# HGRN recurrence and top-k capacity routing on one core: identity products, gate weights, candidate lists and zero writes rearranged

## The chip, the cores and the metric

The kernel runs on one core of one Trainium2 chip. The metric is the device time of one launch in microseconds (us); lower is better. A core has TensorE (PE, with its weight loads PEld), VectorE (DVE), ScalarE (ACT), GpSimd (POOL), and SyncE (SP), which here only issues DMAs; the transfers are done by 16 DMA engines.

## The reference

```python
sig = 1.0 / (1.0 + np.exp(-f_logit))                    # x, f_logit: (4, 5056, 256)
f = lower_bound + (1.0 - lower_bound) * sig
for t in range(S):                                      # per batch row and channel
    h = f[:, t] * h + (1.0 - f[:, t]) * x[:, t]
    y[:, t] = h
x = y.reshape(20224, 256)
logits = x @ w_gate                                     # 8 experts
expert_idx = argmax(logits);  gate_w = softmax(logits)[expert_idx]
out = zeros((20224, 256))
for e in range(8):
    tok_idx = the 80 tokens of expert e with the largest gate_w
    out[tok_idx] = gate_w[tok_idx] * (relu(x[tok_idx] @ w1[e]) @ w2[e])
```

w1 is (8, 256, 1024) and w2 is (8, 1024, 256), all in float32. At most 640 of 20224 rows of the output are not zero, so nearly all of the 20.7 MB that are written are zeros.

## The kernel before

**Scan stage.** A unit n (0 to 39) is 512 time steps of one batch row; a group g is the four batch rows of the same 512 steps, so there are ten groups, and unit n belongs to group n // 4. `OLD = 8` is the last group but one, `LAST = 39` the last unit. The loop at L410 is software-pipelined, and each engine works through its instructions in the order in which the loop emits them. For a unit: `load` (L246) issues two DMAs of 512 KB on SP, f_logit and x, into rings of four buffers; `gate` takes the sigmoid in place on ACT; `enter` multiplies x by it on POOL (unit 0 on DVE); `to_channels` turns both into channel-major PSUM tiles with TensorE transposes ("sp" for f, "up" for x); `decay` writes the decay factors to `h_all` on ACT; `scan` runs two recurrences on DVE, in place in `h_all`; `logits` multiplies by the gate weights `wg`, which `gates` (L242) has scaled once by 1 - lower_bound on DVE.

**Group steps.** Some units after a group is complete, `of_group` hands out its steps one unit at a time: `aside` copies the logits from PSUM on ACT, `by_token` transposes them on TensorE, `maxima` takes the maximum over experts and the difference from it on DVE (tile `cand`), `choice` finds the first best expert on DVE (tiles `eq`, `pick`) and marks it. The last two groups are handled by hand at L423 to L469: `exponentials` on ACT, `halved` (sums over experts by halving, POOL), `worth` (gm = mark minus sum, POOL or DVE), `candidates` (transpose on TensorE, copy on ACT), and `peaks`, which takes the best 8 of each list with MAX8 on DVE. There are `NP` = 8 lists of 128 columns per partition, one per pair of old groups and parity, and the 256 columns of the last two groups are kept whole, so that `fresh` has 64 + 256 = 320 columns.

**Selection.** From L537 DVE takes the best 16 of `fresh`, `spread` and the `rivals` products compare them across partitions, ACT (`signs`, 8 passes) and DVE (two index searches, then `beat`, 4 passes) count who is larger, and the products into `kept` put the 80 tokens of each expert in order. Then ACT, DVE and POOL gather the chosen columns of `h_all`.

**Experts.** `weights` (L492) loads w1 and w2 in halves of 512 KB, 32 of them, into a ring of six, which take the place of the load buffers in memory; the first six are issued at L505. `steps` does 70 steps: a step s below 64 does four matmuls of `hidden` (s = 8 e + c), and from step 6 on also the products of `result` for s - 6. Weight k (from 2 on) is first used at step 2k + 2. Each used-up weight calls `more(1)`, which issues the next weight on SP and then some zeros; the m-th call falls at step 2m + 3 (from the third on) and issues weight m + 5.

**Zeros.** `first_zeros` writes 8 rows per partition (1 MB) from a zeroed tile; it is issued at n = -1. All other zeros are copied inside the output in DRAM by `clear_some(m)`, in quarters of 32 partitions (256 KB); 76 quarters are listed. Before, 20 quarters go out beside the scans at n = 4 to 35, 6 at n = 36 (behind the last load), 30 between the first six weights, and 20 with `more`, the last of them with its 16th call. `scatters` holds back the writes of the experts' rows until all zeros are issued.

**Identity products.** `busy(pool, m, tag)` (L178) issues m products of the identity with itself, two matmul rows of the profile each, into a tile that nobody reads.

On every engine the order of the code is the order of the work: what waits on SP, say, stands in front of all DMAs that the code issues later.

Of the kernel before, what the change touches and what calls it, by code (L numbers as in the profile page):

```python
# [35 lines left out]
def kernel(  # L36
# [94 lines left out]
    parts = [(g, g * P + i) for g in range(0, OLD, 2) for i in range(2)]  # L131
# [26 lines left out]
    def first_zeros(zero):  # L158
        m = ZR * D // ZC
        nc.sync.dma_start(out=out_z[:, :ZR * D].rearrange("p (m z) -> p m z", m=m),  # L160
                          in_=zero.unsqueeze(1).broadcast_to([P, m, ZC]))
# [40 lines left out]
    with tc.tile_pool(name="ld", bufs=4) as ld, \  # L202
# [6 lines left out]
        def setup():  # L209
# [26 lines left out]
            busy(psu, 16, "up")  # L236
# [5 lines left out]
        def gates():  # L242
            for o in range(DC):
                nc.vector.tensor_scalar_mul(wg[:, o], wg[:, o], omlb[:, ds(o, 1)])
# [57 lines left out]
        def aside(g):  # L302
            k = run(g)
            ls = lss[g] = gsm.tile([P, B, P], F32, name="ls", tag="ls")
            if k < P:
                nc.gpsimd.memset(ls[:, :, k:], 0.0)
            nc.scalar.copy(ls[:, :, :k], lgs.pop(g)[:, :, :k])  # L307
# [25 lines left out]
        def choice(g, engine):  # L333
# [5 lines left out]
            nc.vector.tensor_reduce(pick, eq, AX.X, ALU.max)  # L339
            engine.tensor_tensor(marks[:, g], eq, pick.unsqueeze(2).broadcast_to(full),  # L340
                                 ALU.subtract)

# [45 lines left out]
        def peaks(g, tops):  # L388
            for i, (g0, lo) in enumerate(parts):
                if g0 == g:  # L390
                    nc.vector.max(out=tops[:, ds(i * TOP, TOP)], in_=cand[:, lo:(g + 2) * P:2])
# [16 lines left out]
        HALF = OLD // 2  # L408

        for n in range(-AHEAD, n_unit):  # L410
# [3 lines left out]
            elif n == -1:  # L414
                first_zeros(zero)
# [4 lines left out]
            unit(lambda m: to_channels(m, sts, sps, pss, "sp", False), n + 1)  # L420
            unit(lambda m: to_channels(m, uts, ups, psu, "up", True), n + 1)
            unit(decay, n + 1)
            if n == LAST - 2:  # L423
                aside(OLD)
                exponentials(0, OLD)
            elif n == LAST - 1:
                for k in range(0, OLD, HALF):
                    halved(k, HALF)
            unit(scan, n)
            if n == 0:  # L430
                gates()
            some_of(of_group, 1 if n != LAST - 1 else 0)
            unit(logits, n - 1)
            if n + AHEAD == LAST:
                clear_some(6)
            elif B <= n < LAST - AHEAD and (n % 2 or n >= n_unit - 3 * B):
                clear_some(1)
            if n > 0 and n % B == 0:
# [430 lines left out]
```

## Time and profile before

| | us |
|---|---|
| median of 3 runs | 227.79 (226.98 to 228.44) |
| the profiled execution, its own time | 226.11 |
| its span, first to last instruction | 224.2 |
| busy: PE / PEld / DVE / ACT / POOL | 194.8 / 165.1 / 157.7 / 131.6 / 139.8 |
| DMA moved | 80.55 MB, mean 359 GB/s |

The span is 1.9 us shorter than the execution's own time. Busy time is an average over stages with different limits, so the rows further down are taken stage by stage. The stages are: scans to about 129 us, selection to 156 us, experts to 217 us, and the last rows' way out to 224 us.

### The profile page before, as it was taken

The page shows a single profiled execution, that of the slowest core. Times are in us where ns is not written, and L with a number is a line of the kernel's source. Part 1 is how long each engine was busy: PE and PEld are TensorE (multiplying, and loading weights), DVE is VectorE, ACT ScalarE, POOL GpSimd, SP SyncE. Part 2 cuts the span into 40 slices and gives each one's busy share as a digit, 9 for nine tenths or more (in the row PEclk, how much of TensorE's full clock was granted, in tenths as well). Part 3 has the DMA queues.
Part 4 walks back from the last instruction along what each step waited for, and adds up shares of the span by engine and source line. Part 5 has one row for each costly group of instructions (what it writes and reads, how often), then busy time and mean ns, then how long its engine had stood idle before and what let it go on. Part 6 is the DMA issues. An engine that isn't in the chain of part 4 may idle for free.

```text
span 224.2 us, 5701 instructions
## 1 busy us (share of the span) xinstructions
PE 194.8 (87%) x1938; PEld 165.1 (74%) x1938; DVE 157.7 (70%) x487; ACT 131.6 (59%) x367; POOL 139.8 (62%) x279
## 2 busy tenths in 40 slices
PE   7977899998999999999697868989998978989970
PEld 7855678786878787878485648978986856778850
DVE  5398679999999999999978867935686744420010
ACT  4546988879898888877668540428655335330100
POOL 3456988989898989887677760107967710039220
PEclk9999999999999999999999999999999999999998
DMA  6999999999999999999999299999698999999800
GB/s 227 341 417 415 420 420 415 417 421 417 419 416 421 417 421 417 422 415 425 414 418 386 91 324 392 385 361 398 201 292 319 408 400 411 399 379 378 284 21 23
DMA packets 28794, 80.55 MB, mean 359 GB/s; under 512 B 3027, under 2 KB 11349, under 8 KB 26453
## 3 DMA queue, kind: packets, MB, share of 16 engines
q1 hardware_dynamic: 28368, 79.45, 91.3%
q0 software_dynamic: 384, 0.66, 0.8%
q8 instruction: 17, 0.28, 0.5%
q14 instruction: 21, 0.16, 0.2%
q10 hardware_dynamic: 4, 0.00, 0.0%
HBM read 78.39 MB, written 21.36 MB: 445 GB/s over the span
## 4 chain that ended last, share of the span: by engine, by line
DMA 44%; PE 31%; ACT 11%; DVE 4%; POOL 3%; issue 2%; SPq 1%; POOLq 1%; ACTq 0%; DVEq 0%
DMA f_t<-in_f_logit_dram 21%; DMA w_sb<-in_moe_w_dram 11%; DMA x_t<-in_x_dram 9%; PE warm L181 7%; PE h_ps L707 6%; PE y_ps L722 6%; PE sp L266 5%; ACT h_all L276 4%; DMA out_dram<-out_dram 3%; ACT f_t L255 3%; PE lg L299 3%; PE up L266 3%; ACT ls L307 2%; ACT signs L565 2%; POOL xe L675 1%
## 5 line engine op out<-in xcount | busy, mean ns | idle before, releaser
L259 POOL TENSOR_TENSOR x_t<-f_t,x_t 128x1024 f32<-128x1024 f32 x39 | 93.5, 2401 | 21.3 <-DMA x_t<-in_x_dram 14.7
L284 DVE TENSOR_TENSOR_SCAN h_all<-h_all,up 128x512 f32<-128x512 f32 (+1 forms) x80 | 94.6, 1240 | 3.8 <-ACT h_all L276 2.5
L276 ACT ACTIVATE h_all<-sp,nomlb 128x512 f32<-128x512 f32 (+1 forms) x80 | 50.0, 676 | 7.9 <-PE sp L266 7.7
L255 ACT ACTIVATE f_t<-f_t 128x1024 f32<-128x1024 f32 x40 | 42.5, 1062 | 19.9 <-DMA f_t<-in_f_logit_dram 19.5
L266 PE MATMUL up<-ident,x_t 128*128 128x128 f32 x320 | 42.4, 276 | 6.3 <-POOL x_t L259 5.6
L707 PEld LDWEIGHTS h_ps<-xt,w_sb 128*128 128x128 f32 x256 | 37.0, 191 | 12.4 <-issue 5.2
L266 PE MATMUL sp<-ident,f_t 128*128 128x128 f32 x320 | 43.8, 280 | 1.5 <-ACT h_all L276 1.5
L266 PEld LDWEIGHTS up<-ident,x_t 128*128 128x128 f32 x320 | 35.3, 140 | 10.1 <-POOL x_t L259 9.3
L266 PEld LDWEIGHTS sp<-ident,f_t 128*128 128x128 f32 x320 | 34.4, 141 | 9.5 <-issue 6.9
L707 PE MATMUL h_ps<-xt,w_sb 128*128 128x80 f32 x256 | 36.5, 268 | 4.9 <-DMA w_sb<-in_moe_w_dram 3.9
L722 PE MATMUL y_ps<-w_sb,hid 128*80 128x256 f32 x128 | 37.3, 381 | 0.0
L675 POOL COPY xe<-h_all 128x8 uint8 x192 | 26.2, 197 | 12.8 <-issue 8.2
L299 PE MATMUL lg<-h_all,wg 128*32 128x128 f32 (+1 forms) x640 | 26.5, 282 | 4.3 <-ACT ls L307 3.1
L675 DVE COPY xe<-h_all 128x8 uint8 x256 | 20.9, 162 | 11.4 <-issue 11.3
L181 PE MATMUL warm<-ident 128*128 128x128 f32 x188 | 24.9, 298 | 1.4 <-POOL ident masks.py:199 1.4
L181 PEld LDWEIGHTS warm<-ident 128*128 128x128 f32 x188 | 24.3, 213 | 1.7 <-POOL ident masks.py:199 1.4
L716 ACT ACTIVATE hid<-h_ps 128x320 f32<-128x320 f32 x16 | 7.0, 437 | 31.1 <-PE h_ps L707 28.4
L740 POOL DMA_INDIRECT out_dram<-y,goal x8 | 7.6, 951 | 28.0 <-DMA w_sb<-in_moe_w_dram 18.8
L299 PEld LDWEIGHTS lg<-h_all,wg 128*32 128x32 f32 x640 | 15.4, 108 | 11.3 <-ACT ls L307 5.1
L675 ACT COPY xe<-h_all 128x8 uint8 x192 | 20.2, 193 | 5.4 <-issue 3.4
L722 PEld LDWEIGHTS y_ps<-w_sb,hid 128*80 128x80 f32 x128 | 14.8, 152 | 0.8
L737 DVE TENSOR_SCALAR y<-y_ps,gsl 80x256 f32<-80x256 f32 x8 | 3.8, 476 | 16.2 <-PE y_ps L722 16.2
(125 smaller groups left out, 97.2 us busy)
## 6 DMA issues: line engine op xcount, KB each, us to landing
f_t<-in_f_logit_dram SPq DMA_DIRECT2D x40, 512.0 KB, 6.6
x_t<-in_x_dram SPq DMA_DIRECT2D x40, 512.0 KB, 6.8
w_sb<-in_moe_w_dram SPq DMA_DIRECT2D x32, 512.0 KB, 7.9
out_dram<-out_dram SPq DMA_DIRECT2D x35, 256.0 KB, 7.1
out_dram<-out_dram SPq DMA_DIRECT2D x4, 1024.0 KB
out_dram<-out_dram SPq DMA_DIRECT2D x6, 512.0 KB, 14.8
out_dram<-out_dram SPq DMA_DIRECT2D x3, 768.0 KB
out_dram<-zero SPq DMA_DIRECT2D x1, 1024.0 KB
```

Source lines behind the costliest of these rows:

```text
L181: nc.tensor.matmul(warm, ident, ident, start=True, stop=True)
L255: nc.scalar.activation(s_t, s_t, ACT.Sigmoid, scale=-1.0)
L259: (nc.gpsimd if n else nc.vector).tensor_tensor(u_t, sts[n], u_t, ALU.mult)
L266: nc.tensor.transpose(at, src[n][:, r, ds(o * P, P)], ident)
L276: nc.scalar.activation(columns(n, o).rearrange("c (p r) -> c p r", r=R), sps.pop((n, o)).rearrange("c (r p) -> c p r", r=R) [:, lead(n // ...
L284: nc.vector.tensor_tensor_scan(h, h, ups.pop((n, o))[:, lead(n // B):], columns(n - B, o)[:, size(n // B - 1) - 1:] if n >= B else 0.0, AL ...
L299: nc.tensor.matmul(lgs[g][ds(r * LC, LC), b, :k], wg[:, o], h[:, r], start=o == 0, stop=o == DC - 1, skip_group_check=True)
L675: copy(xe[:, :, ds(WORD * (k + j), WORD)], pair(v - HOME))
L707: nc.tensor.matmul(HP[e, i][:, c], w[1, e, i][:, o, ds(c * P, P)], XT[e][:, o], start=o == 0, stop=o == DC - 1, skip_group_check=True)
L716: nc.scalar.activation(HID[e][:, ds(i * CH, CH)], HP.pop((e, i)), ACT.Relu)
L722: nc.tensor.matmul(YP[e], HID[e][:, c], w[2, e, c // CH][:, c % CH], start=c == 0, stop=c == FC - 1)
L740: one = nc.gpsimd.indirect_dma_start(out=out, out_offset=bass.IndirectOffsetOnAxis(ap=goal[:, ds(e, 1)], axis=0), in_=Y.pop(e), in_offset= ...
```

## The change

Nine edits, by the diff:

- The identity products fall from 16 to 9 at the start (`setup`), from 4 to 3 ahead of the last group's transposes, and from 32 to 10 ahead of the selection; 20 and 22 stay where they were.
- `gates` runs on ACT in place of DVE, and is emitted at n = -1 in place of n = 0.
- `first_zeros` is cut into four quarters, emitted at n = 0 to 3, behind that turn's load.
- Beside the scans a quarter goes out at every third unit, n = 5, 8, ... 35: 11 in place of 20.
- Behind the last load (n = 36) 10 quarters in place of 6.
- Between the first six weights 5, 5, 6, 6, 6, 6 in place of 5 each: 34 in place of 30. With `more` one each, so 21 in place of 20 are left for it, the last with the 21st call.
- Group OLD: its `aside` moves from n = 37 to 36, its `by_token` between the transposes of n = 37, its `maxima` behind the scan of n = 37. Its mark goes to POOL, its sums to DVE (before: `halved` on POOL).
- The last group: `aside` in two parts, three units ahead of the last logits and one behind. All four `worth` of old groups on POOL, half of `halved` put off to there, and the order of `candidates`, `by_token` and `peaks` is new.
- Four lists of 256 columns (one per half of the old groups and parity) in place of eight of 128; `fresh` has 288 columns.

```diff
     assert OLD % 4 == 0 and size(OLD) == G and OLD == n_grp - 2
-    parts = [(g, g * P + i) for g in range(0, OLD, 2) for i in range(2)]
+    HALF = OLD // 2
+    parts = [(g, g * P + i) for g in range(0, OLD, HALF) for i in range(2)]
     NP = len(parts)
...
     zeros = [(k, q) for k in clears[1:] for q in range(ZQ)]
-    def first_zeros(zero):
+    def first_zeros(zero, q=0, n=ZQ):
         m = ZR * D // ZC
-        nc.sync.dma_start(out=out_z[:, :ZR * D].rearrange("p (m z) -> p m z", m=m),
-                          in_=zero.unsqueeze(1).broadcast_to([P, m, ZC]))
+        rows = ds(q * QP, n * QP)
+        nc.sync.dma_start(out=out_z[rows, :ZR * D].rearrange("p (m z) -> p m z", m=m),
+                          in_=zero[rows].unsqueeze(1).broadcast_to([n * QP, m, ZC]))
     def clear(k, q=0, m=ZQ):
...
             nc.vector.tensor_tensor(before, before, mates, ALU.mult)
-            busy(psu, 16, "up")
+            busy(psu, 9, "up")
             lb_t = plg.tile([P, DC], F32, name="lb_t", tag="lt")
...
             for o in range(DC):
-                nc.vector.tensor_scalar_mul(wg[:, o], wg[:, o], omlb[:, ds(o, 1)])
+                nc.scalar.activation(wg[:, o], wg[:, o], ACT.Identity, scale=omlb[:, ds(o, 1)])
         def load(n):
...
                                      start=o == 0, stop=o == DC - 1, skip_group_check=True)
-        def aside(g):
+        def aside(g, lo=0, hi=B):
             k = run(g)
-            ls = lss[g] = gsm.tile([P, B, P], F32, name="ls", tag="ls")
-            if k < P:
-                nc.gpsimd.memset(ls[:, :, k:], 0.0)
-            nc.scalar.copy(ls[:, :, :k], lgs.pop(g)[:, :, :k])
+            if lo == 0:
+                lss[g] = gsm.tile([P, B, P], F32, name="ls", tag="ls")
+                if k < P:
+                    nc.gpsimd.memset(lss[g][:, :, k:], 0.0)
+            nc.scalar.copy(lss[g][:, lo:hi, :k], lgs[g][:, lo:hi, :k])
         def by_token(g):
...
             maxima(g)
-        def choice(g, engine):
+        def chosen(g):
             eq = gsm.tile([P, C, E], F32, name="eq", tag="eq")
...
             nc.vector.tensor_reduce(pick, eq, AX.X, ALU.max)
+            return eq, pick
+
+        def mark(g, eq, pick, engine):
             engine.tensor_tensor(marks[:, g], eq, pick.unsqueeze(2).broadcast_to(full),
                                  ALU.subtract)
+
+        def choice(g, engine):
+            mark(g, *chosen(g), engine)
         def exponentials(g0, g1, aside=False):
...
                 if g0 == g:
-                    nc.vector.max(out=tops[:, ds(i * TOP, TOP)], in_=cand[:, lo:(g + 2) * P:2])
+                    nc.vector.max(out=tops[:, ds(i * TOP, TOP)], in_=cand[:, lo:(g + HALF) * P:2])
         def unit(f, m):
...
         LAST = n_unit - 1
-        HALF = OLD // 2
         for n in range(-AHEAD, n_unit):
...
                 nc.sync.dma_start(out=wg[:, :, :E], in_=w_gate.rearrange("(o p) e -> p o e", p=P))
-            elif n == -1:
-                first_zeros(zero)
+            elif 0 <= n < ZQ:
+                first_zeros(zero, n, 1)
             if n == -AHEAD:
...
             unit(lambda m: to_channels(m, sts, sps, pss, "sp", False), n + 1)
+            if n == LAST - 2:
+                by_token(OLD)
             unit(lambda m: to_channels(m, uts, ups, psu, "up", True), n + 1)
             unit(decay, n + 1)
-            if n == LAST - 2:
-                aside(OLD)
+            if n == -1:
+                gates()
+            elif n == LAST - 2:
                 exponentials(0, OLD)
             elif n == LAST - 1:
-                for k in range(0, OLD, HALF):
-                    halved(k, HALF)
+                halved(0, HALF)
             unit(scan, n)
-            if n == 0:
-                gates()
-            some_of(of_group, 1 if n != LAST - 1 else 0)
+            if n == LAST - 2:
+                maxima(OLD)
+            some_of(of_group, 1)
             unit(logits, n - 1)
+            if n == LAST - 3:
+                aside(OLD)
             if n + AHEAD == LAST:
-                clear_some(6)
-            elif B <= n < LAST - AHEAD and (n % 2 or n >= n_unit - 3 * B):
+                clear_some(10)
+            elif B < n < LAST - AHEAD and n % 3 == 2:
                 clear_some(1)
-            if n > 0 and n % B == 0:
+            if n > 0 and n % B == 0 and n // B <= OLD:
                 g = n // B - 1
-                of_group += ([[lambda g=g: aside(g)]] if g < OLD else [])
-                of_group += [[lambda g=g: shifted(g)], [lambda g=g: choice(g, nc.gpsimd if g < OLD else nc.vector)]]
+                of_group += [[lambda g=g: aside(g)], [lambda g=g: shifted(g)],
+                             [lambda g=g: choice(g, nc.gpsimd)]]
         assert not of_group
+        g = n_grp - 1
+        aside(g, 0, B - 1)
+        best = chosen(OLD)
         exponentials(OLD, OLD + 1)
         logits(LAST)
-        g = n_grp - 1
-        aside(g)
-        busy(psu, 4, "up")
+        aside(g, B - 1, B)
+        worth(0, 0, 2, nc.gpsimd)
+        worth(2, 0, 2, nc.gpsimd)
+        mark(OLD, *best, nc.gpsimd)
+        sums(OLD, OLD + 1)
+        candidates(0)
+        busy(psu, 3, "up")
+        candidates(2)
         by_token(g)
-        for k in (0, 2, HALF):
-            worth(k, k // HALF * HALF, 2, nc.gpsimd)
-        worth(OLD - 2, HALF, 2, nc.vector)
-        for k in (0, 2, OLD - 2, HALF):
-            candidates(k)
+        halved(HALF, HALF)
+        worth(HALF, HALF, 2, nc.gpsimd)
+        worth(HALF + 2, HALF, 2, nc.gpsimd)
+        worth(OLD, OLD, 1, nc.gpsimd)
         assert OLD == 8
...
         choice(g, nc.vector)
-        halved(OLD, 1)
-        worth(OLD, OLD, 1, nc.gpsimd)
-        turned(OLD, 1, fresh[:, ds(NP * TOP, P)])
+        candidates(HALF)
         sums(g, g + 1)
         worth(g, g, 1, nc.vector)
+        candidates(HALF + 2)
+        turned(OLD, 1, fresh[:, ds(NP * TOP, P)])
         turned(g, 1, fresh[:, ds(NP * TOP + P, P)])
-        busy(psu, 32, "up")
-        for k in (2, OLD - 2, HALF):
-            peaks(k, fresh)
+        busy(psu, 10, "up")
+        peaks(HALF, fresh)
         nc.scalar.copy(cand[:, OLD * P:], fresh[:, NP * TOP:])
...
         w_sb[key] = weights(*key)
-        clear_some(5)
+        clear_some(6 if len(w_sb) > 2 else 5)
     far = consts.tile([K, E], F32, name="far")
...
                     w[key] = weights(*key)
-                    clear_some(1 + (len(late) % 4 == 0))
+                    clear_some(1)
                 del late[:m]
...
```

## Rows read from the trace of the kernel before

**Rows 1.** Chain that ended last, shares of the span by engine.

```profile
DMA 44%; PE 31%; ACT 11%; DVE 4%; POOL 3%; issue 2%; SPq 1%; POOLq 1%; ACTq 0%; DVEq 0%
```

**Rows 2.** Windows: stretch, us, busy PE PEld DVE ACT POOL, clock, DMA share, GB/s.

```profile
20.00:94.00 74.00, 69.94 (x865) 58.49 (x866) 68.52 (x75) 61.91 (x85) 64.49 (x33) 1.00 1.02 418
94.00:122.00 28.00, 24.35 (x293) 19.55 (x291) 25.84 (x28) 19.81 (x28) 21.46 (x11) 1.00 1.03 420
...
124.00:128.00 4.00, 3.54 (x70) 2.94 (x72) 3.90 (x6) 2.64 (x4) 2.51 (x5) 1.00 0.10 29
128.00:157.00 29.00, 24.45 (x222) 22.62 (x219) 19.32 (x87) 11.79 (x73) 10.11 (x49) 1.00 1.01 371
157.00:160.00 3.00, 3.00 (x28) 2.96 (x28) 2.23 (x26) 2.94 (x28) 3.00 (x24) 1.00 0.35 97
160.00:172.00 12.00, 11.55 (x82) 9.70 (x80) 9.07 (x94) 6.20 (x46) 9.12 (x67) 1.00 0.89 294
172.00:198.00 26.00, 22.10 (x149) 17.96 (x150) 13.06 (x138) 10.88 (x86) 6.61 (x48) 1.00 1.05 404
```

**Rows 3.** Timeline of the start: start us, us, engine, line, operation, tiles, count.

```profile
1.41 6.66 PE L181 MATMUL warm<-ident 128*128 128x128 f32 x32 [1.41 <-POOL ident masks.py:199]
...
8.40 1.22 DVE L259 TENSOR_TENSOR x_t<-f_t,x_t 128x1024 f32<-128x1024 f32 x1
...
12.68 1.71 DVE L244 TENSOR_SCALAR wg<-wg,omlb 128x32 f32<-128x32 f32 x2
...
15.77 1.06 ACT L255 ACTIVATE f_t<-f_t 128x1024 f32<-128x1024 f32 x1 [3.26 <-DMA f_t<-in_f_logit_dram]
```

**Rows 4.** Timeline of one group's scans, and line L335 (min/median/max ns).

```profile
55.63 0.29 DVE L325 TENSOR_REDUCE mx<-lt 128x16 f32<-128x128 f32 x1 [0.51 <-PE lt L313]
...
59.15 5.96 DVE L284 TENSOR_TENSOR_SCAN h_all<-h_all,up 128x512 f32<-128x512 f32 x5
...
L335 DVE SCALAR_TENSOR_TENSOR eq<-cand,revexp x10: 264/666/1719, 36.0 to 133.3; 128x128 f32<-128x128 f32 x10
```

**Rows 5.** Timeline, end of the scans: last x product, group OLD's maxima, last scans.

```profile
122.04 2.36 POOL L259 TENSOR_TENSOR x_t<-f_t,x_t 128x1024 f32<-128x1024 f32 x1 [0.61 <-DMA x_t<-in_x_dram]
...
124.07 0.29 DVE L325 TENSOR_REDUCE mx<-lt 128x16 f32<-128x128 f32 x1 [1.28 <-PE lt L313]
...
124.60 4.25 DVE L284 TENSOR_TENSOR_SCAN h_all<-h_all,up 128x448 f32<-128x448 f32 x4
```

**Rows 6.** Timeline of SP: first weight, and the first weight behind a used-up one.

```profile
126.53 0.38 SPq L496 DMA_DIRECT2D w_sb<-in_moe_w_dram  x1
...
158.36 0.37 SPq L500 DMA_DIRECT2D w_sb<-in_moe_w_dram  x1
```

**Rows 7.** Timeline of the selection: identity products, MAX8 lists, rivals, ranks.

```profile
135.26 7.31 PE L181 MATMUL warm<-ident 128*128 128x128 f32 x64
135.46 1.99 DVE L391 MAX8 fresh<-cand 128x8 f32<-128x128 f32 x6 [0.42 <-PE fresh L380]
...
138.03 0.50 DVE L542 MAX8 vals<-fresh 128x8 f32<-128x320 f32 x1 [0.58 <-ACT last_of L472]
...
139.75 0.36 DVE L550 TENSOR_TENSOR spread<-vals,place 128x192 f32<-128x192 f32 x1
...
142.41 0.82 PE L555 MATMUL rivals<-spread,mates 128*128 128x192 f32 x4
...
147.29 0.17 DVE L586 COPY rank<-by_act 128x8 f32<-128x8 f32 x1 [1.65 <-ACT signs L565]
```

**Rows 8.** Chain that ended last, in order of time: start us, us, what.

```profile
156.32 2.90 PE h_ps L707 x24
...
197.67 0.64 PE h_ps L707 x4
...
214.24 3.04 PE y_ps L722 x14
```

**Rows 9.** Windows (columns as in the second group), TensorE idle at the end.

```profile
222.00:223.00 1.00, 0.00 (x0) 0.00 (x0) 0.00 (x0) 0.00 (x0) 0.00 (x0) 0.70 0.00 0
```

## The prediction

> **What bounds the kernel now.** I read the chain of waits first: DMA holds 44% of it, TensorE 31%, and DVE, the busiest engine beside TensorE in the scans, only 4% [rows 1]. Then the windows by stage [rows 2]. In the scans the DMA share is full and the rate is 418 to 420 GB/s, while DVE is busy 68.52 of 74 and 25.84 of 28 us: transfers set the pace, with DVE close behind. From 124 to 128 the DMA engines are nearly empty (29 GB/s): the last load and the six quarters behind it are through, and the first weight is not issued until 126.53 [rows 6], because it takes over load buffers that the transposes of unit 39 still read. From 128 to 157 they are full again at 371 GB/s with six weights and 30 quarters. From 157 to 160 they are nearly empty (97), to 172 half fed (294), then full (404) to 198. In that last stretch TensorE waits for weights; the last such wait ends at 197.67, and from there it runs through to 217.28 [rows 8]. So the time is a sum of transfers and of holes between them, plus a TensorE tail. The selection chain between 129 and 156 is on the path only because the DMA engines have run dry when the experts start: the first weight behind a used-up one goes out at 158.36 [rows 6].
>
> **The head.** Seven identity products fewer are 14 of 32 rows, 14/32 x 6.66 = 2.9 us, and unit 0's product on DVE waited for the constants behind them until 8.40 [rows 3]. The two gate instructions hold DVE for 1.71 us and leave it; on ACT each costs between 0 and 1.06, the price of the far larger sigmoid [rows 3], so 2.1 at most, hidden in the 3.26 us that ACT then waits for unit 3's f [rows 3]; without this cover unit 2's decay would come that much later. That wait is what counts: 1 MB of zeros stands ahead of this load, and at 418 GB/s it is 2.5 us. Issued behind units 3 to 6 in quarters, it lets unit 3 in some 2.5 us sooner. The bytes remain, so this gain only helps DVE; for DMA it is nothing. The first copied quarter reads what n = 0 wrote; should SP make it wait for all four, the loads behind it wait too, between 0 and the 2.5 us that they take; I take 0, as the copy is issued two units after the fourth.
>
> **The scans.** Nine quarters fewer are 9 x 0.262 = 2.36 MB, at 420 GB/s 5.6 us, if the last x lands ahead of the quarters issued behind it. If these share the engines evenly with it, four more of them take back 1.05 MB: 1.31 MB, 3.1 us. DVE must keep up: it idled 5.5 and 2.2 us in the two windows, 7.7 in all, plus the 1.71 of the gates, so its work doesn't exclude either value. Between 3.1 and 5.6 I take 4.0, below the middle, since DVE is at 93%: the last x, ready for POOL at 122.04 [rows 5], lands 4.0 sooner.
>
> **Group OLD.** Its transposes stood ahead of unit 39's own in TensorE's queue, waiting for a copy on ACT that came late; DVE idled 1.28 us for them [rows 5]. From the end of POOL's last product (122.04 + 2.36 = 124.40) to the weight's issue are 2.13 us, which bound this gain from above; below it is zero, if the transposes, now put ahead of "up" of unit 38, stop that instead. I take 1.0. The first weight goes out at 126.53 - 4.0 - 1.0 = 121.5.
>
> **First weights and 34 quarters.** By the windows the bytes flow again 1.5 us after the issue (126.53 to 128). 6 x 0.524 + 34 x 0.262 = 12.06 MB at 371 GB/s are 32.5 us: 123.0 to 155.5.
>
> **The selection.** Scans end at 124.60 + 4.25 = 128.85 [rows 5], experts start at 156.32 [rows 8]. With the new order I get: scans 4.0 sooner, and half of group OLD's 1.28, 0.6; the lists: six MAX8 in 1.99 us (0.33 each) stood at the end of the candidates [rows 7], now two of 256 columns, by interpolation between 0.33 for 128 and 0.50 for 320 (bounds) 0.44 each, 1.1 less; the steps that change engines or order (two "worth", a mark and "halved" on POOL, a sum on DVE, the last copy in two parts, one identity product fewer) have no row in this order: bounded by a loss and a gain of the 1.28 that such a wait cost group OLD, I take a gain of 1.2, nearest to it, since the last copy is now a quarter and two lists are done early; the identity products: 7.31 us became 10/32 of it, 2.3, and "spread" was ready at 140.11 while the rivals' product began at 142.41, so 2.3 less. Not all of that shows: ACT's eight passes were last (DVE waited 1.65 at the rank copy [rows 7]), and once rivals come 2.3 sooner, DVE's own searches are, so 1.65 of the 2.3 and a little more. Sum 4.6 + 1.1 + 1.2 + 1.7 = 8.6: experts start near 147.7. This is ahead of the transfers by 7.8 us (155.5), so most of it is not on the path any more. Where it goes is the filling of the holes: weight 6 is asked for, some 2 us after the start as before, with DMA still busy, and the rows at 97 and 294 GB/s become full ones.
>
> **The experts.** With 21 quarters, the last weight with zeros ahead of it is number 26, not 21. Up to it go 21 x 0.524 + 20 x 0.262 = 16.25 MB; at 404 GB/s 40.2 us, and 1.5 from issue side to landing: 155.5 + 41.7 = 197.2. Two steps of TensorE per weight and quarter (0.786 MB, 1.95 us) are 1.7 us, by the 20 steps between 197.67 and 214.24, so transfers stay ahead of TensorE's need by nothing and set the pace. Behind weight 26 TensorE runs through: before, the tail from weight 21 was 19.6 us; ten steps of 0.84 fewer leave 11.2. End 208.4, against 217.28: 8.9 less. Zeros now end one expert later, so the rows of five experts are scattered together; this starts near 198 and is hidden by the 11 us of TensorE; without that cover, the end waits for them. The rest (224.2 - 217.3) stays.
>
> **Sum.** 226.11 - 8.9 = 217.2. The profiled execution was 1.7 below the median of the runs; I add half of that and say 218.0.
>
> **A rule against the change.** With TensorE idle from 217.3 on, its granted clock is 0.70 of full in the window at 222, between the levels of 2.4 and 1.2 GHz; before that every window shows 1.00 [rows 2, 9]. The Trainium skill's "TensorE: Matmul & The Clock Gate" (Part 1, what's actually happening) says that the throttled state is the default and that activity releases it. The trace agrees. By this rule the identity products are no waste, and 22 fewer of them ahead of the rivals could leave the selection's products at half clock; the third rival prices that.
>
> **Rivals.**
> (1) *DVE sets the pace of the scans.* The eq step of line 335 takes 264 to 1719 ns, median 666, for the same work, beside POOL's product of 2.36 us [rows 4, 5]; a group's other DVE work is dense (five scans in 5.96 us, a wait of 0.51 at the maxima). When transfers no longer pace POOL, eq may wait longer. The scans then gain nothing from fewer bytes: first weight at 125.5, end 8.9 - 4.0 = 4.9 less, 222. If each of nine eq steps waits for a whole product (2.36 - 0.67 more), that is 15 us of DVE work, which the 7.7 idle, the gates' 1.7 and the head's 2.5 take up but for 3: 225. The page "SBUF — State Buffer" (SBUF: two separate sides) states an exclusive lock on a port pair that DVE and GpSimd share, held for the whole instruction; the spread of line 335 agrees.
> (2) *Slower: the experts' transfers stay half fed.* If asking one weight and one quarter per used-up weight is what kept 160 to 172 at 294 GB/s, not the empty ring, then 16.25 MB take 55.3 us, 15.1 more: 226.1 - 8.9 + 15.1 = 232. It decides from 16.25 / (40.2 + 8.9) = 331 GB/s down. For it speaks that row; against it that the same pattern with 1.25 quarters ran at 404 from 172, and that DMA now enters the stage with 7.8 us of work waiting. Around 350 (6.2 us more) the result would be within 1% to 1.5%.
> (3) *The clock falls* behind the ten identity products. At half clock the steps up to 14 (about 10 us) take 10 more; the selection's 7.8 us of slack takes up most: 2 to 3 us on the path, 220.
>
> **How the numbers follow.** Forecast 0.66; rival 1 0.17; rival 2 0.13, of which 0.07 slower by over 1%, 0.06 within 1%; rival 3 0.04. One per cent is about what a measurement of this kernel can tell from no change. Within 1% also takes 0.03 of rival 1. So faster 0.84, same 0.09, slower 0.07. The forecast's own range: 3.1 to 5.6 for 4.0, 0 to 2.13 for 1.0, and 371 and 404 GB/s each uncertain by 3% (2.2 us together) give 213 to 222; it reaches to 223.5 to take in most of rival 1.
>
> **What would show it.** Right: DMA share full from 20 to past 190 but for one hole of 2 to 4 us ahead of the first weight; first weight near 121.5; experts' start near 148 with no fall of GB/s behind it; last wait for a weight near 197, and 11 us of TensorE behind it. Wrong: eq of line 335 well over 1 us in most groups with DVE at 98% (rival 1); 290 GB/s in the 12 us behind the experts' start (rival 2); a granted clock under 1.00 between 130 and 170 (rival 3); a last wait that is not for a weight.

## The result and the profile after

The changed kernel took 217.0 us, median of 4 runs (216.23 to 217.38), the kernel before 227.4 beside it; the ratio is 0.954 (95% interval 0.948 to 0.960). The forecast was 218.0, between 213 and 223.5. Ratios, here and below, leave out executions more than 1.5% above the fastest of their kernel. The profiled execution took 217.36 us with a span of 215.5. All times within a span below are of profiled executions.

The chain that ended last, shares by engine, of the changed kernel (the profile follows it back to 127.58 only, so these are shares of a part):

```profile
DMA 19%; PE 11%; DVE 5%; POOL 2%; POOLq 1%; issue 1%; ACT 0%; SPq 0%; DVEq 0%; ACTq 0%
```

Windows of the changed kernel (columns as in [rows 2]):

```profile
20.00:94.00 74.00, 68.61 (x855) 57.72 (x853) 66.76 (x75) 60.88 (x85) 64.17 (x33) 1.00 1.02 416
...
118.00:120.00 2.00, 1.78 (x16) 1.49 (x14) 1.68 (x2) 1.99 (x3) 1.04 (x1) 1.00 0.95 324
120.00:122.00 2.00, 1.27 (x40) 0.93 (x40) 1.43 (x2) 1.50 (x4) 1.75 (x5) 1.00 0.67 166
124.00:148.00 24.00, 18.93 (x159) 17.06 (x157) 16.46 (x81) 11.34 (x76) 9.39 (x48) 1.00 1.01 368
148.00:157.00 9.00, 9.00 (x70) 8.23 (x69) 6.71 (x74) 5.91 (x49) 8.37 (x62) 1.00 1.01 352
157.00:160.00 3.00, 1.68 (x12) 1.22 (x11) 2.03 (x19) 0.21 (x1) 1.60 (x13) 1.00 0.96 359
160.00:172.00 12.00, 11.09 (x75) 8.80 (x74) 8.23 (x92) 5.71 (x44) 8.32 (x61) 1.00 1.05 402
172.00:198.00 26.00, 23.50 (x160) 19.37 (x160) 7.99 (x74) 8.71 (x63) 3.28 (x24) 1.00 1.05 402
```

The holes of [rows 2] are mostly closed: where 124 to 128 had moved 29 GB/s there is one short dip ahead of 122, and the 97 and 294 GB/s of 157 to 172 are 359 and 402. A shallow dip is left behind the new start of the experts, from 152 to 160:

```profile
152.00:156.00 4.00, 4.00 (x31) 3.54 (x30) 3.25 (x37) 2.56 (x23) 4.00 (x31) 1.00 0.94 315
156.00:160.00 4.00, 2.68 (x19) 2.12 (x17) 2.89 (x26) 0.66 (x6) 1.97 (x17) 1.00 1.01 347
```

As far as the chain is followed, it has no transfer ahead of the experts any more.

The end of the scans (issue of the last x, sigmoid of the last f, last x product, first weight's issue, last scans), the timeline to set beside [rows 5, 6]:

```profile
108.89 0.33 SPq L253 DMA_DIRECT2D x_t<-in_x_dram  x1
...
115.53 1.06 ACT L257 ACTIVATE f_t<-f_t 128x1024 f32<-128x1024 f32 x1
...
116.67 2.37 POOL L261 TENSOR_TENSOR x_t<-f_t,x_t 128x1024 f32<-128x1024 f32 x1 [0.94 <-ACT f_t L257]
...
120.26 0.39 SPq L514 DMA_DIRECT2D w_sb<-in_moe_w_dram  x1
...
120.57 2.18 DVE L286 TENSOR_TENSOR_SCAN h_all<-h_all,up 128x448 f32<-128x448 f32 x2 [0.90 <-ACT h_all L278]
```

The issue of the last x in the kernel before:

```profile
113.30 0.33 SPq L251 DMA_DIRECT2D x_t<-in_x_dram  x1
```

The selection, to set beside [rows 7]:

```profile
128.69 2.40 PE L183 MATMUL warm<-ident 128*128 128x128 f32 x20
128.96 0.91 DVE L400 MAX8 fresh<-cand 128x8 f32<-128x256 f32 x2 [0.49 <-PE fresh L389]
...
132.00 0.36 DVE L568 TENSOR_TENSOR spread<-vals,place 128x192 f32<-128x192 f32 x1
...
132.57 0.89 PE L573 MATMUL rivals<-spread,mates 128*128 128x192 f32 x4 [1.48 <-issue]
...
137.82 0.17 DVE L604 COPY rank<-by_act 128x8 f32<-128x8 f32 x1
```

The chain in order of time, to set beside [rows 8]:

```profile
146.89 2.90 PE h_ps L725 x24
...
151.57 8.91 DMA w_sb<-in_moe_w_dram
...
183.87 8.46 DMA w_sb<-in_moe_w_dram
...
192.46 0.64 PE h_ps L725 x4
...
206.00 3.04 PE y_ps L740 x14
```

The first weight goes out 6.27 us sooner than before, the experts start 9.43 sooner, and TensorE ends at 209.04 in place of 217.28, 8.24 sooner.

### The profile page after: what moved, and what is told of

Same layout as the page of the kernel before. It is cut to its first block, busy times and chain, and to the rows that moved or that the text cites. A ratio compares the mean times of both kernels' runs of the same rounds, so it can differ in the third digit from the quotient of the medians.

```text
span 215.5 us, 5581 instructions
## 1 busy us (share of the span) xinstructions
PE 187.8 (87%) x1878; PEld 158.2 (73%) x1878; DVE 150.7 (70%) x479; ACT 131.4 (61%) x370; POOL 139.1 (65%) x279
## 5 line engine op out<-in xcount | busy, mean ns | idle before, releaser
L261 POOL TENSOR_TENSOR x_t<-f_t,x_t 128x1024 f32<-128x1024 f32 x39 | 92.3, 2374 | 16.4 <-DMA x_t<-in_x_dram 11.0
L268 PE MATMUL sp<-ident,f_t 128*128 128x128 f32 x320 | 44.6, 283 | 0.1
L268 PEld LDWEIGHTS sp<-ident,f_t 128*128 128x128 f32 x320 | 35.0, 143 | 8.2 <-issue 5.5
L693 DVE COPY xe<-h_all 128x8 uint8 x256 | 20.8, 163 | 11.5 <-issue 11.4
L183 PE MATMUL warm<-ident 128*128 128x128 f32 x128 | 17.2, 298 | 1.4 <-POOL ident masks.py:199 1.4
L183 PEld LDWEIGHTS warm<-ident 128*128 128x128 f32 x128 | 16.6, 212 | 1.5 <-POOL ident masks.py:199 1.4
```

The lines of the kernel that those rows point to most:

```text
L183: nc.tensor.matmul(warm, ident, ident, start=True, stop=True)
L261: (nc.gpsimd if n else nc.vector).tensor_tensor(u_t, sts[n], u_t, ALU.mult)
L268: nc.tensor.transpose(at, src[n][:, r, ds(o * P, P)], ident)
L693: copy(xe[:, :, ds(WORD * (k + j), WORD)], pair(v - HOME))
```

## Experiments

Each kernel ran beside the kernel before on the same chip. "Gain" is (1 - ratio) x 227; the next three columns are from the profile: issue of the first weight, start of the experts, end of TensorE.

| kernel | median | ratio (95%) | gain | first weight | start | TensorE ends |
|---|---|---|---|---|---|---|
| before | 227.4 | | | 126.53 | 156.32 | 217.28 |
| after | 217.0 | 0.954 (0.948 to 0.960) | 10.5 | 120.26 | 146.89 | 209.04 |
| e1 | 220.6 | 0.976 (0.969 to 0.984) | 5.4 | 125.71 | 152.23 | 212.37 |
| e2 | 220.0 | 0.973 (0.965 to 0.982) | 6.1 | 120.75 | 152.18 | 211.47 |
| e3 | 219.1 | 0.968 (0.961 to 0.976) | 7.2 | 120.35 | 151.25 | 211.11 |
| e4 | 225.1 | 0.992 (0.987 to 0.997) | 1.8 | 120.34 | 157.39 | 217.09 |
| e5 | 211.7 | 0.936 (0.930 to 0.942) | 14.6 | 120.35 | 147.09 | 203.03 |
| e6 | 218.8 | 0.964 (0.957 to 0.971) | 8.2 | 120.68 | 147.39 | 210.76 |
| e7 | 226.0 | 0.996 (0.992 to 1.000) | 1.0 | | | |
| e8 | 217.9 | 0.962 (0.956 to 0.967) | 8.7 | 121.46 | 148.56 | 210.15 |
| e9 | 228.5 | 1.009 (1.004 to 1.013) | -2.0 | 121.98 | 152.26 | 220.79 |
| e10 | 216.4 | 0.956 (0.952 to 0.960) | 9.9 | 120.55 | 148.39 | 208.87 |
| e11 | 223.4 | 0.986 (0.980 to 0.992) | 3.2 | 126.66 | 155.67 | 216.31 |
| e12 | 227.8 | 1.006 (1.002 to 1.010) | -1.3 | 132.12 | 158.78 | 221.07 |

### Which part gives what: e1, e2, e11, e7

e1 is the changed kernel with the zeros where they were:

```diff
-            elif 0 <= n < ZQ:
-                first_zeros(zero, n, 1)
+            elif n == -1:
+                first_zeros(zero)
...
-                clear_some(10)
-            elif B < n < LAST - AHEAD and n % 3 == 2:
+                clear_some(6)
+            elif B <= n < LAST - AHEAD and (n % 2 or n >= n_unit - 3 * B):
...
-        clear_some(6 if len(w_sb) > 2 else 5)
+        clear_some(5)
...
-                    clear_some(1)
+                    clear_some(1 + (len(late) % 4 == 0))
```

> The changed kernel with the zeros where they were before (1 MB ahead of unit 3's load, 20 quarters beside the scans, 6 behind the last load, 30 between the first weights, 20 with later weights); all else as changed. Theory (transfers and the holes between them set the end): the first weight goes out near 125.5 us, the earlier experts' start (near 152) fills most of the hole behind the first weights, and the end lies about 6 us ahead of the kernel before, near 220.5 us. Rival (the zeros matter little, the shorter selection carries the gain): within 1.5 us of the changed kernel, 217 to 218.5.

e2 is the kernel before with these lines the other way round, the zeros alone:

> The kernel before with nothing but the new places of the zeros. Theory: first weight near 121.5, transfers of the first weights and 34 quarters end near 156, the experts start near 151, still ahead of that, so nearly the whole gain is there: 218 to 219 us. Rival (the experts' start sets the end, so the selection carries most of the gain): it starts 4 us later than in the changed kernel, 221 us.

e11 is the kernel before with 9, 3 and 10 identity products in place of 16, 4 and 32:

```diff
-            busy(psu, 16, "up")
+            busy(psu, 9, "up")
...
-        busy(psu, 4, "up")
+        busy(psu, 3, "up")
...
-        busy(psu, 32, "up")
+        busy(psu, 10, "up")
```

> The kernel before with the fewer identity products of the change (9 instead of 16 at the start, 3 instead of 4, 10 instead of 32 ahead of the rivals) and nothing else. Theory: before is limited by the experts' start (start + 60.96 = end), so 22 products fewer show in it: rivals 2 to 4 us sooner, start near 153, 224 to 225.5. Rival (the products were hidden in before too, since ACT's passes or the transfers end last): 226.5 to 228.

e7 is the changed kernel with both the zeros of e1 and the products of before, so that only the order of the steps, the four lists and the gates on ACT stay:

> The changed kernel with the zeros and the identity products of the kernel before; what stays of the change is the order of the last groups' steps, the four lists of 256 and the gates on ACT. Theory (the end is the later of two lines: first weight + 88.7, and experts' start + 59.7): the first weight goes out near 125.5, group OLD's gain of 0.9 less than before, and the experts start near 154 to 155; zeros as before put 1.25 quarters behind a weight, so the start's line is that of before, start + 60.9, 215.5; about 225 us, 2 to 3 less than before. Rival (the order does nothing without the other parts): not under 226.5 us.

e1 came out as expected (220.6 us). e2, at 220.0, is a microsecond above its 218 to 219: the experts start at 152.18, not 151, and a start as late as that sets the end (next section).

Zeros alone gain 6.1 us, everything else 5.4, and both together 10.5. So about 1 us of 11.5 is lost between them, less than the intervals of some 2 us can tell from none. Of the rest, the identity products alone gain 3.2 (interval 1.9 to 4.6), a little more than expected (223.4 us against 224 to 225.5); in e11's profile, of an execution of 224.4 us, the rivals start 2.0 us sooner than in [rows 7], at 140.39, the granted clock falls to 0.50 between 140 and 146, the experts start 0.65 sooner, and the end is 1.0 sooner. e7 is inconclusive: 1.0, with an interval from 0 to 1.9, lies between theory and rival (its profiled execution took 227.7 us, 1.7 above its median, and isn't read here). Whether the zeros or the rest are worth more, the intervals don't tell. In e2 the first weight goes out 5.8 us sooner and the experts start 4.1 sooner, with nothing changed in between: both come from the earlier end of the scans.

### How late the experts may start: e3, e4, e10

e3 is the changed kernel with the identity products of before, e4 has 60 in place of the ten ahead of the rivals, e10 none there:

```diff
-        busy(psu, 10, "up")
+        busy(psu, 60, "up")
```

> The changed kernel with the identity products as before (16 at the start, 4, and 32 ahead of the rivals); all else as changed. The rivals' products then start about 3.9 us later and the ranks about 3.3 us later. Theory: the experts start 3.3 us later, which lies inside their lead of some 8 us over the transfers, so the time stays within 1 us of 217. Rival (selection on the path): 220 us.

> The changed kernel with 60 identity products in place of 10 ahead of the rivals' products, which makes the experts start about 10 us later (near 157). Theory: their lead of 8 us over the transfers is used up, the hole behind the first weights comes back, and the end moves by 3 to 5 us, to 220 to 222. Rival (selection on the path): 10 us, 227.

> The changed kernel without the ten identity products ahead of the rivals' product. Theory: these products lie inside the wait for the lists; the rivals' product still starts at 132.5 give or take 0.5, the granted clock falls in the stretch 128 to 138 and costs the selection under 1 us, which the 2.4 us of lead take up: 216.5 to 218. Rival (the clock stays low into the experts' first steps, whose steps then pace the requests for weights): a clock under 0.9 after 147, weights late as in the kernel with 13 quarters, 219 or more.

The three, with the changed kernel, are doses of one thing. The first weight stays within 0.3 us, the start of the experts moves. From 146.89 to 148.39 (e10) the end doesn't move (209.04, 208.87). At 151.25 (e3) it is 2.07 later, at 157.39 (e4) 8.05 later. In the last two, end minus start is 59.86 and 59.70: from there on each microsecond counts. Their mean, 59.8, reaches back from 209.04 to a start of about 149.3. So the changed kernel's selection has some 2.4 us to spare, not 7.8, and the expectations for e3 (within 1 us of 217) and e4 (220 to 222) both failed: 219.1 and 225.1.

The chains of e10, e3 and e4, and windows of e3 and e4:

```profile
148.39 2.90 PE h_ps L724 x24
...
205.83 3.04 PE y_ps L739 x14
```
```profile
151.25 2.90 PE h_ps L725 x24
...
208.07 3.04 PE y_ps L740 x14
```
```profile
157.39 2.91 PE h_ps L725 x24
...
214.05 3.04 PE y_ps L740 x14
```
```profile
148.00:152.00 4.00, 3.45 (x32) 3.26 (x30) 2.24 (x26) 4.00 (x42) 4.00 (x30) 1.00 1.03 410
152.00:156.00 4.00, 4.00 (x35) 3.80 (x34) 2.89 (x33) 2.93 (x28) 4.00 (x30) 1.00 0.79 250
156.00:160.00 4.00, 4.00 (x31) 3.61 (x30) 2.82 (x35) 2.57 (x19) 4.00 (x31) 1.00 0.94 320
160.00:164.00 4.00, 4.00 (x30) 3.42 (x30) 2.81 (x22) 1.50 (x12) 1.88 (x16) 1.00 0.84 278
```
```profile
156.00:160.00 4.00, 3.45 (x31) 3.26 (x30) 2.05 (x23) 4.00 (x41) 4.00 (x31) 1.00 0.02 6
160.00:164.00 4.00, 4.00 (x31) 3.60 (x31) 2.74 (x33) 2.26 (x19) 4.00 (x31) 1.00 0.81 251
164.00:168.00 4.00, 4.00 (x31) 3.57 (x30) 3.31 (x35) 2.17 (x18) 2.86 (x22) 1.00 0.95 319
168.00:172.00 4.00, 4.00 (x31) 3.56 (x30) 2.75 (x30) 2.11 (x17) 3.11 (x24) 1.00 0.87 300
```

In e4 the ring, that is the first six weights and the 34 quarters among them, has run dry when the experts start, and the three windows behind are again at 251 to 319 GB/s, with TensorE busy throughout and one weight and one quarter asked for at a time, as at 294 before [rows 2]. In e3 the ring's last transfers are still under way at the start (410 GB/s to 152), and yet 152 to 164 runs at 250 to 320. In the changed kernel, where requests queue behind the ring's rest, 160 to 172 runs at 402. So the pattern of requests alone does not half-feed the transfers; how much of the ring is left does. The bytes bear it out: set against a steady 402 GB/s from 152 to 172, the changed kernel loses 1.4 us of transfers, e3 3.9 and e4 9.5, that is 2.5 and 8.1 more, and their ends are 2.07 and 8.05 later. Why a start on an empty ring stays near 300 GB/s for 12 us, though the requests of that stretch come every 1.9 us (159.44 to 170.89 for six intervals) and so ask for 0.786 / 1.9 = 412, was not separated further; ACT and POOL gather in part of the same stretch, and no run moves that work alone.

e10 also prices the clock. Two windows of its selection, and from its timeline and chain the rivals' products and the identity products behind them:

```profile
130.00:132.00 2.00, 0.00 (x0) 0.00 (x0) 1.35 (x5) 0.44 (x2) 0.00 (x0) 0.50 1.00 365
...
134.00:136.00 2.00, 2.00 (x11) 2.00 (x10) 1.97 (x6) 1.90 (x8) 0.00 (x0) 0.50 1.02 402
```
```profile
132.83 1.62 PE L572 MATMUL rivals<-spread,mates 128*128 128x192 f32 x4 [3.71 <-DVE spread L567]
134.45 5.67 PE warm L183 x40
```

With TensorE idle, the granted clock falls to 0.50, the lower level of 1.2 GHz; the rivals' products take 1.62 us in place of 0.89, the 40 rows behind them 5.67 in place of 4.63, the experts start 1.5 later (0.3 of it stands there already ahead of the rivals, where `spread` comes at 132.26 in place of 132.00), and the 2.4 us to spare take it up: 216.4 us, just under the 216.5 to 218 expected. The selection was expected to lose under 1 us. So even the last ten products gain nothing that can be measured.

### The transfers' side: e5, e6, e8

e5 leaves out the 21 quarters behind the late weights (that part of the output is not written); e6 issues 13 quarters behind the last load in place of 10:

```diff
-                    clear_some(1)
+                    del zeros[:1]
```
```diff
-                clear_some(10)
+                clear_some(13)
```

> The changed kernel without the 21 quarters that go out with later weights: these rows of the output are never zeroed. Theory, as mended by the first four runs (the end is the later of two lines: first weight plus the transfers up to weight 26 plus TensorE's rest, or experts' start plus 59.7): the first line loses 21 x 0.262 MB at 0.40, 13.7 us, so TensorE never waits for long, and from a start at 146.9 it needs about 54.5: end of TensorE at 201.5, the time near 209.5 us. Rival (TensorE or the gathers set the stage): within 1 us of 217.

> The changed kernel with 13 quarters behind the last load in place of 10, so 18 in place of 21 with later weights. Theory: the engines run short between 118 and 122 us and take 2 to 3 more quarters there without holding up the first weight; the transfers in the experts' stage shrink by 0.79 MB, 2.0 us, and the last weight behind zeros is number 23: 1.2 to 1.8 us less, 215.3 to 215.8. Rival (they hold up the last load or the first weights instead): 217 or more.

e8 is the changed kernel with its start as before: 16 identity products in `setup`, the gates on DVE at n = 0, the first zeros whole at n = -1.

> The changed kernel with the start as before: 16 identity products, the gate weights scaled on DVE behind unit 0's scans, and the 1 MB of first zeros ahead of unit 3's load; all else as changed. Theory (transfers pace the scans, and their bytes are the same): the first weight goes out 0 to 1 us later, the time is 217 to 218. Rival (DVE paces the scans, so its head start of 2.5 to 4.5 us counts): 219.5 to 221.5.

e5 takes 5.3 us less than the changed kernel by the medians, 4.1 by the ratios, and ends 6.0 sooner in the profile, with the same start. Its windows:

```profile
160.00:172.00 12.00, 12.00 (x88) 10.40 (x88) 8.40 (x95) 6.44 (x51) 8.47 (x62) 1.00 0.93 320
172.00:198.00 26.00, 26.00 (x188) 23.17 (x188) 8.28 (x73) 8.62 (x56) 8.95 (x30) 1.00 0.94 326
```

TensorE is busy 38 of 38 us and asks for no more than 326 GB/s; in the changed kernel the same windows have it at 34.59 of 38 with DMA at 402. Transfers do pace the experts, and without the zeros in between TensorE does, 55.9 us from start to end; 54.5 were expected, and 209.5 us where 211.7 were measured. e8 bears out the same line: first weight 1.2 later, end 1.1 later, although its experts' start (148.56) is within the spare time. So, with the zeros where the change puts them, the end is the later of two: first weight + 88.7 (88.78 after, 88.69 e8, 88.32 e10) and experts' start + 59.8. The start of the kernel itself matters by about as much as it delays the first weight.

e6 put 0.79 MB more where a dip is, and came out at 218.8 us, about 2 more than the changed kernel, where 215.3 to 215.8 were expected. Its windows, and the wait for weight 6 from its chain:

```profile
118.00:120.00 2.00, 1.78 (x24) 1.36 (x16) 2.00 (x3) 1.97 (x3) 1.46 (x1) 1.00 1.03 328
120.00:122.00 2.00, 1.55 (x38) 1.13 (x36) 1.13 (x2) 1.81 (x4) 1.34 (x3) 1.00 1.00 315
...
154.00:160.00 6.00, 3.90 (x29) 3.39 (x27) 4.40 (x42) 2.18 (x18) 3.98 (x31) 0.98 1.01 314
160.00:172.00 12.00, 11.94 (x63) 9.98 (x64) 6.47 (x66) 3.87 (x27) 5.82 (x44) 0.73 1.05 401
```
```profile
149.44 10.49 DMA w_sb<-in_moe_w_dram
```

The dip was smaller than three quarters: the DMA engines are full there now, from 118 to 122 only 0.3 MB more go through than in the changed kernel, and weight 6 lands 10.49 us after its issue. TensorE idles 2.1 of the 6 us ahead of 160 (in the changed kernel it is 1.3), its clock falls, and the next 12 us run at a mean of 0.73. e6 ends at 210.76, later than either of the two lines gives (120.68 + 88.7 = 209.4), though three quarters fewer stand behind the late weights. So the lines hold only while the clock does in the experts' first steps; how much of the loss is the late weight and how much the clock, no run separates.

### What a quarter of zeros costs: e9, e12

e9 writes all zeros from a zeroed tile of 256 columns (1 KB runs) in place of copying them inside DRAM; e12 cuts the quarters into 16 partitions with 16 KB runs in place of 32 with 8 KB (of e9 only the line of the copy is shown; it also moves tiles to make room for the zeroed one):

```diff
-        nc.sync.dma_start(out=out_z[rows, ds(k * D, n)], in_=out_z[rows, :n])
+        nc.sync.dma_start(out=out_z[rows, ds(k * D, n)].rearrange("p (m z) -> p m z", z=ZC),
+                          in_=zero[rows].unsqueeze(1).broadcast_to([m * QP, n // ZC, ZC]))
```
```diff
-    ZR = 8
+    ZR = 16
...
-    ZQ = 4
+    ZQ = 8
...
-            elif B < n < LAST - AHEAD and n % 3 == 2:
+            elif B < n < LAST - AHEAD and n % 4 == 2:
```

> The changed kernel with the zeros written from a zeroed tile in SBUF (1 KB runs) in place of copies inside the output in DRAM; same places, same bytes written. If the rate of 368 GB/s with many zeros, against 402 to 416 with few, comes from reading DRAM as well as writing it, the stretch of the first weights gets 2 to 4 us shorter; the experts' start then sets the end (206.6 in place of 209.0), so 2 to 2.5 us less, near 214.7. If the rate does not depend on where zeros are read: 217. If short runs cost more than the reading: slower than 218.

> The changed kernel with quarters of zeros cut the other way: 16 partitions with runs of 16 KB each instead of 8 KB, the first 2 MB of zeros written in eight parts; 8 quarters beside the scans, 10 behind the last load, 14 behind the weights' loads and 20 late. If the number of runs is what makes stretches with many zeros slow (368 GB/s against 415), the ring passes in 2 to 4 us less and the start sets the end: 214 to 215.5. If it is the copying of zeros itself, 216.5 to 218.

(In e12 34 quarters stand behind the first weights' loads, as in the changed kernel; the 14 of the text is a slip.) A window of e9, and one of e12 over its own ring stage:

```profile
124.00:148.00 24.00, 20.17 (x162) 18.20 (x162) 14.69 (x48) 8.36 (x40) 7.20 (x26) 0.93 1.00 304
```
```profile
36.00:40.00 4.00, 1.29 (x18) 0.86 (x19) 0.00 (x0) 1.54 (x2) 0.30 (x1) 0.50 0.09 32
...
134.00:160.00 26.00, 20.38 (x181) 18.19 (x173) 18.16 (x87) 12.25 (x79) 11.26 (x54) 1.00 1.01 379
```

e9's ring runs at 304 GB/s against 368, so the copy inside DRAM is the cheaper way, at these runs. e12 failed by a wait of its own: with eight parts of first zeros, the last goes out at n = 7, and the zeroed tile shares its buffer with the logits' copies `ls`. This is the row of e12's waits that shows it:

```profile
ACT ls L310 <- DMA out_dram<-zero: 9.7, 1, 9.7
```

ACT holds its place in order, so f's sigmoid and all behind it stop, and DMA runs dry from 36. That is the 11 us by which e12 misses. Its ring stage is readable all the same: 379 GB/s against 368 over the like stretch, 3% or 1 us in 33. Longer runs could bring 1 us here, not the 2 to 4 expected; but this is one profile, of an execution of 230.1 us with a median of 227.8, and a version of e12's cut without that wait was not tried, so the 1 us is not shown. No kernel here that writes the whole output beat the changed one by what can be measured.

## Why the prediction was right, and where it wasn't

**Last x and first weight.** The prediction took 4.0 sooner, between 3.1 (shared engines) and 5.6 (in order). The last x product starts at 116.67 in place of 122.04, 5.4 sooner, and it no longer waits for x: its wait is for the sigmoid of f on ACT. The last x itself was issued 4.4 sooner (108.89 in place of 113.30) and had landed at most 7.8 us later, with ten quarters behind it; before, with six, 8.7 us lie between its issue and the product that waited for it. By the semaphore counts in the traces it landed at 115.83 in place of 121.88, 6.0 sooner, even past the upper bound. So the quarters behind the last load don't hold it up, and the last 0.6 is lost on ACT. The Trainium skill's "DMA: Bandwidth & Descriptors" (Queues, rings and completion order) says that each engine consumes its descriptors in ring order; the trace agrees, as the load with ten quarters behind it was under way no longer than the one with six, and had the prediction used it, the upper bound would have been the value. The reason given for staying below the middle, DVE at 93%, was the misjudged part: DVE's work shrank beside it (rival 1 below). Group OLD was forecast at 1.0: from the product's end at 119.04 to the issue are 1.22 in place of 2.13 us, 0.9. Together the first weight came at 120.26, forecast 121.5.

**Ring.** Forecast 371 GB/s throughout; measured 368, and 352 in its last 9 us.

**Selection.** Forecast 8.6 sooner, start 147.7; measured 9.43, 146.89. The scans end 6.1 sooner (122.75) in place of 4.6, so the lists, the order and the products together gave 3.3, not 4.0; no run splits them. MAX8 of 256 took 0.455 (0.91 for two), interpolated 0.44. The ranks were ready 9.5 us sooner than in [rows 7], with DVE's searches last, as forecast.

**The lead: the step that failed.** "This is ahead of the transfers by 7.8 us (155.5), so most of it is not on the path any more." Measured, what the selection may lose is 2.4 (e3, e4, e10). The prediction took the end of the ring's transfers as the point up to which a later start costs nothing. But a start at that point finds the ring empty, and then come the slow windows that the prediction itself counted as filled: (404 - 97) x 3 + (404 - 294) x 12 GB/s x us are 2.24 MB, 5.5 us at 404. This has to be covered by the lead as well: 7.8 (155.5 to 147.7) less 5.5 leave 2.3, a sum made after the runs. The forecast of the time didn't suffer, as the start stood on the right side of the edge; the prediction had not worked out where the edge was, so that was luck. It called the shorter selection mostly off the path, when the fewer identity products (30, of which 22 ahead of the rivals) are worth 3.2 alone (e11), and 2.1 to 3.3 in the changed kernel (e3, by the profile and by the ratios).

**Experts.** Forecast were full transfers at 404 GB/s, a last wait near 197.2 and TensorE's end at 208.4; measured 402, and 209.04. The last wait in the chain ends earlier, at 192.46, for weight 23 and not 26; weight 26 is needed six steps of 0.84 later, at 197.5, and is there. Of the sum's two halves, the first weight came 1.2 sooner than forecast and the stretch from it to TensorE's end was 1.9 longer (88.8 against 86.9); that they nearly cancel, and 8.9 stands against 8.24, is luck. About 1.2 of the 1.9 can be put down to the dip from 152 to 160: 315 and 347 GB/s, where the forecast had 371 up to 155.5 and 404 behind it.

**Tail and outside.** From TensorE's end to the span's were 6.9 us before and are 6.5; the five experts' scatters are hidden as forecast.

**Rival 1**, DVE paces the scans: refuted. The line of eq in the changed kernel, beside [rows 4]:

```profile
L338 DVE SCALAR_TENSOR_TENSOR eq<-cand,revexp x10: 265/268/739, 34.9 to 126.4; 128x128 f32<-128x128 f32 x10
```

Its median fell from 666 to 268 ns instead of rising, DVE's busy time from 20 to 94 from 68.52 to 66.76. It goes with the zeros' places and not with the rest of the change: 680 ns in e1, where the zeros stand as before, and 328 in e2, which moves them alone. That the long values came of meeting POOL's product still fits; no experiment moved that product alone.

**Rival 2**, transfers half fed by the pattern of requests: refuted, as the same pattern ran at 402 GB/s from 160. But its rate is near: e4, whose ring is empty at the start, is at 290 from 160 to 172.

**Rival 3**, the clock falls behind ten products: no window of 2 us of the changed kernel from 20 to 198 is under 1.00. In e1 to e6, e8 and e9, though, it fell between 128 and 138, to 0.50 to 0.54 in the lowest window of 2 us. With ten products that moved the rivals by 0.2 us (e5, 132.79 against 132.57); in e8, where it lasts to 136, their products take 1.46 us in place of 0.89. With 32 it adds to their price: 8.5 to 8.9 us in place of the 7.31 of [rows 7], and the rivals start at 137.27 (e3). A window of e3:

```profile
128.00:130.00 2.00, 1.43 (x8) 1.35 (x8) 1.20 (x4) 0.12 (x1) 0.00 (x0) 0.51 0.99 394
```

The price forecast, 2 to 3 us, was too high for a fall in the selection: e10, at half clock from 130 to 136, lost 1.5 on the start and nothing at the end. A fall in the experts' first steps, which the rival also counted, stands in e6 and e9; e6 ends 1.7 later than the changed kernel.

## What to carry to other kernels

Where one stage prefetches for the next, the time that the first may lose is, in this kernel, not the time until its last transfer lands: it is that, less what the next stage loses when it starts on an empty queue. The second could be read from the windows of before (5.5 us). The end is then the later of two lines, and doses (a few identity products more or less) show which line holds. Products that only keep an engine busy ahead of a chain have to earn their time: here ten or none made no difference, and 30 more (22 of them ahead of the rivals) cost 2 to 3 us.

## What the runs showed of the hardware

- Transfers queued behind a load didn't delay it: with ten quarters issued behind the last x it had landed at most 7.8 us after its issue, with six before 8.7.
- Copies of zeros inside DRAM, behind the last load and nearly alone on the engines, move 315 to 328 GB/s at a full DMA share (e6, 118 to 122), mixed with weights 368, while the scans' loads with single quarters among them run at 416 to 418; zeros from the tile in 1 KB runs give 304 in the mix. The place of a quarter, beside loads or by itself, changes its cost.
- Between 128 and 138 the granted clock was 1.00 in the profiles of before and after and fell to 0.50 to 0.54 in nine experiments (e1 to e6, e8 to e10), of which four (e5, e6, e8, e9) have the changed kernel's code in that stretch. The Trainium skill's "TensorE: Matmul & The Clock Gate" (Part 1, what's actually happening) ties the throttled state to lack of activity; e10, idle from 130 to 132 and at 0.50, agrees. Why it fell in e5, e6, e8 and e9, where the ten products stood in that stretch as in the changed kernel, is left open.
